# DeltaNet and soft-MoE slots: 32-token steps with wider matmul tiles and half as many matmuls

## The chip, the cores and the metric

The kernel runs on one core of one Trainium2 chip. The metric is device time in microseconds, as the median of several runs. The engines have short names throughout: PE is TensorE (matmuls; its weight loads are listed apart as PEld), DVE is VectorE, ACT is ScalarE, POOL is GpSimd, SP is SyncE, which here only issues DMAs.

## The reference

Two blocks follow each other. The first is a delta-rule attention with a state of 48x48 per batch and head, 4 batches, 8 heads, 768 tokens, all in 32-bit floats:

```python
k_n = k / (np.linalg.norm(k, axis=-1, keepdims=True) + 1e-06)
for t in range(S):
    kt, vt, bt = (k_n[:, :, t], v[:, :, t], beta[:, :, t, None])
    y[:, :, t] = np.einsum('bhd,bhde->bhe', q[:, :, t], state)
    v_old = np.einsum('bhde,bhd->bhe', state, kt)
    state = state + bt[:, :, :, None] * np.einsum('bhd,bhe->bhde', kt, vt - v_old)
```

Its output, as x of 3072 tokens by 384 features, goes through a mixture of experts with 32 slots (8 experts, 4 slots each, hidden width 1024):

```python
logits = x @ phi
d = softmax(logits, axis=0)          # over the tokens
slot_input = d.T @ x                 # 32 x 384, four rows per expert
slot_out[e] = relu(slot_input[e] @ w1[e]) @ w2[e]
c = softmax(logits, axis=1)          # over the slots
return c @ slot_out
```

(The two softmaxes stand here in short; the reference writes them out, with 1e-9 added to the sums.)

## The kernel before, in words

**Layout.** The partitions hold 4 batches x 32 tokens. A step is 32 tokens of all four batches and all eight heads; there are 24 steps, and four steps make a group, so there are 6 groups. Head vectors of 48 are padded with zeros to 64, so that two heads fill 128 partitions after a transpose. `e` counts pairs of heads, `g` the head in the pair, `b` the batch, `c` the step in its group, `m` the group.

**One step's preparation.** `load` (L315) brings K, Q and V, each with four DMAs of 48 KB on SP's queue, into rings of 11, 5 and 7 buffers. `turn` (L346, copied to X by ACT at L355) transposes K and Q. `products` (L373) multiplies K by K and K by Q, within each batch: 32 matmuls with tiles of 48x32. ACT copies the first to G (L385), DVE masks the second into AT (L389).

**One group's inversion.** `invert` takes the G of four steps: a 32x32 block transpose on DVE (lb, L404), norms, an elimination on POOL within blocks of 16 (L443, L447; on DVE for the first group), a transpose back to DT (L459) and to Dn (L461), and then two rounds of small matmuls that join the two halves of 16 tokens, `couple`: 128 matmuls each (L473, L478). ACT copies the first result to X16 (L486), DVE subtracts the second from DT (L493).

**One step's chain.** `chain` is the serial part. `state` multiplies the transposed K by the state St (R, L518), DVE subtracts this from V (L534), `solve` multiplies by DT (W, L544), ACT and DVE copy the result in two masked versions, one for even and one for odd batches, side by side into W (L557, L553), `update` adds K times W to the state, which stays in two banks of PSUM (S, L567; 64 tokens of two batches at a time), and ACT and DVE copy one bank each to St (L582, L579). Beside it run Q times the state (QS, L518) and the inner product AT times W (AU, L590), which give the output Y (L597). `state`, `solve` and `inner` are 32 matmuls each.

**Routing.** After each group `route` transposes Y (L615), forms logits (L628), updates a running maximum and the slot sums sacc (L688 to L698). At the end `experts` runs the slots through w1 (L863) and w2 (L903) and writes the output (L938 on). 24 pieces of w1 (512 KB) and 32 of w2 (384 KB) are loaded by SP at L755 into whatever buffer is free for good (`weights`, `home`, `place`), and into nine buffers `wx` of their own; the last w2 pieces overwrite w1 pieces that have been used.

**Order.** The program is emitted in an order that a planner finds by hand-written costs. `Plan.op` notes an operation with its engine, its time and what it reads and writes; `Plan.order` runs a list schedule and picks, among the ready operations of an engine, the one with the longest path behind it. It also models the clock of TensorE, by windows of TICK, and six free banks of PSUM. Each engine then runs its instructions strictly in the planned order. Every 32-bit matmul appears in the profile as two matmul records and two weight loads.

Of the kernel before, what the change touches and what calls it, by code (L numbers as in the profile page):

```python
# [15 lines left out]
class Op:  # L16
    __slots__ = ("eng", "us", "fn", "deps", "succ", "acq", "rel", "bias", "land", "tail", "start", "end", "left", "at", "name", "area")
# [9 lines left out]
class Plan:  # L27
# [9 lines left out]
    TICK, NEED = 3.413, 0.374  # L37

    def __init__(self, banks, limit):
        self.ops, self.writer, self.readers = [], {}, {}  # L40
        self.free = {b: 0.0 for b in range(banks)}
        self.limit = limit

    def op(self, eng, us, fn, r=(), w=(), acq=None, rel=None, pre=(), bias=0.0, land=0.0, name=""):
        o = Op()
        us, o.area = us if isinstance(us, tuple) else (us, 0.0)
# [40 lines left out]
    def order(self):  # L87
# [9 lines left out]
        tick, full, sums = 0, False, {}  # L97
        while len(done) < n:
            picks = []
            for eng, ls in ready.items():  # L100
# [15 lines left out]
                if cand:  # L116
                    first = min(c[0] for c in cand)
                    t, o = min(((t, o) for t, o in cand if t <= first + 1e-9), key=lambda c: (-c[1].tail, c[1].at))
                    picks.append((t, o.at, o))
# [16 lines left out]
            if o.eng == "PE":  # L136
                while (tick + 1) * self.TICK <= t:
                    full = sums.get(tick, 0.0) >= self.NEED * self.TICK
                    tick += 1
                us *= 1.0 if full else 2.0  # L140
                x, e = t, t + us
                while x < e:
                    k = int(x / self.TICK + 1e-9)
                    y = min(e, (k + 1) * self.TICK)
                    sums[k] = sums.get(k, 0.0) + o.area * (y - x) / us
                    x = y
# [28 lines left out]
def kernel(  # L175
# [56 lines left out]
    AT = ring(NA, [P, 2, HQ, C], "AT")  # L232
# [5 lines left out]
    DT = ring(2, [P, U, C], "DT")  # L238
    Dn = buf([P, U, C], "Dn")
    X16 = buf([P, U, QC], "X16")  # L240
    R = buf([P, H, D], "R")
    W = ring(2, [P, H, 2, D], "W")
    St = buf([P, 2, HQ, 2, D], "St")
# [16 lines left out]
    def pe(n, m, cols, conc, area=None):  # L260


        us = n * 2 * max(20, (2 * max(min(64, m), cols) + 12) / conc) / 2400
        return us, n * 2 * cols * 2 * (area or 1.0 / conc) / 2400

    def turns(n):
        return 0.113 * n, 128 * 2 * n / 2400
# [29 lines left out]
    tri = buf([P, C], "tri")  # L297
    nc.vector.tensor_reduce(tri, bdm.rearrange("p h t -> p t h"), axis=AX.X, op=ALU.add)
# [9 lines left out]
    nc.gpsimd.memset(Dn, 0.0)  # L308
    nc.vector.memset(bank[:, 6:8, :], 0.0)
# [50 lines left out]
    def products(n, which):  # L360
# [6 lines left out]
        def product():  # L367
            for e in range(HQ):
                for b in range(B):
                    for g in range(2):  # L370
                        r = slice(DP * g, DP * g + D)
                        rb = slice(C * b, C * b + C)
                        nc.tensor.matmul(  # L373
                            at(h, g)[rb, w * C * e:w * C * (e + 1)], lhsT=x[r, 0, e, rb],
# [3 lines left out]
        plan.op("PE", pe(32, 32, w * C, 6.0, 0.125), product,  # L378
                r=[("X", n % NX, i) for i in {0, *which}], w=[h], acq=h,
                pre=[("G", m % 2, c)] * (0 in which) + [("AT", n % NA)] * (1 in which), name="prod")  # L380
        for j, i in enumerate(which):
            ps = lambda j=j: at(h, 0, 2)[:, :, 0:w * C * HQ].rearrange(
                "p g (e j t) -> p g e j t", e=HQ, j=w)[:, :, :, j, :]
            if i == 0:
                plan.op("ACT", act(256), lambda ps=ps: nc.scalar.activation(  # L385
                    G[m % 2][:, H * c:H * c + H].rearrange("p (e g) t -> p g e t", g=2), ps(),
                    ACT.Copy), r=[h], w=[("G", m % 2, c)], rel=h, name="G")
            else:
                D_(dve(256, True), lambda ps=ps: nc.vector.tensor_tensor(  # L389
                    AT[n % NA], ps(),  # L390
                    tri.unsqueeze(1).unsqueeze(1).broadcast_to([P, 2, HQ, C]), op=ALU.mult),
                   r=[h], w=[("AT", n % NA)], rel=h, name="AT")

# [3 lines left out]
    def invert(m):  # L397
# [56 lines left out]
        for s in range(2):  # L454
# [3 lines left out]
                op=ALU.mult), r=["tt", "tt1", ("gm", z)], w=["tS"], name="tS")  # L458
        D_(dve(1024, False, 1.75), lambda: nc.vector.transpose(  # L459
            DT[z].rearrange("p u t -> p t u"), tS), r=["tS"], w=[("DT", z)], name="DT")  # L460
        D_(dve(512, False, 1.75), lambda: nc.vector.transpose(  # L461
            Dn.rearrange("p u s -> p s u")[:, 0:QC, :],
            tS.rearrange("p t s -> p s t")[:, 0:QC, :]), r=["tS"], w=["Dn"], name="Dn")

        hx, ht = Banks(1, "bulk"), Banks(1, "bulk")

        def couple(us, first):
            for u in us:
                for b in range(B):
                    r0 = C * b  # L470
                    if first:
                        r = slice(r0, r0 + C)
                        nc.tensor.matmul(at(hx)[r0:r0 + QC, QC * u:QC * u + QC],  # L473
                                         lhsT=gr[r, u, 0:QC], rhs=DT[z][r, u, QC:C],
                                         start=(u == 0), stop=True, skip_group_check=True)
                    else:
                        r = slice(r0, r0 + QC)
                        nc.tensor.matmul(at(ht)[r0:r0 + C, QC * u:QC * u + QC],  # L478
                                         lhsT=Dn[r, u, :], rhs=X16[r, u, :],
                                         start=(u == 0), stop=True, skip_group_check=True)  # L480

        for i in range(4):
            plan.op("PE", pe(32, 32, 16, 4, 0.0625),
                    lambda i=i: couple(range(8 * i, 8 * i + 8), True),
                    r=gk + [("DT", z)], w=[hx], acq=hx, pre=["X16"], name="X16")
        plan.op("ACT", act(512), lambda: nc.scalar.activation(  # L486
            X16.rearrange("p u t -> p (u t)"), at(hx), ACT.Copy), r=[hx], w=["X16"], rel=hx,
            name="X16")
        for i in range(4):
            plan.op("PE", pe(32, 32, 16, 4, 0.0625),  # L490
                    lambda i=i: couple(range(8 * i, 8 * i + 8), False),
                    r=["X16", "Dn"], w=[ht], acq=ht, name="T16")
        D_(dve(512, True), lambda: nc.vector.tensor_tensor(  # L493
            DT[z][:, :, QC:C], DT[z][:, :, QC:C], at(ht).rearrange("p (u t) -> p u t", t=QC),
            op=ALU.subtract), r=[ht, ("DT", z)], w=[("DT", z)], rel=ht, name="DT-")
# [11 lines left out]
    def chain(n):  # L507
        m, c = divmod(n, GC)
        x, kk, a, t = X[n % NX], K[n % NK], AT[n % NA], DT[m % 2]
        vn, ww, y = V[n % NV], W[n % 2], Y[m % 2]  # L510

        def state(h, i):
            for e in range(HQ):
                for b in range(B):
                    for g in range(2):
                        r = slice(DP * g, DP * g + D)
                        rb = slice(C * b, C * b + C)
                        nc.tensor.matmul(at(h, g)[rb, D * e:D * e + D], lhsT=x[r, i, e, rb],  # L518
                                         rhs=St[r, b // 2, e, b % 2, :], start=(e == 0),
                                         stop=(i == 0), skip_group_check=True)  # L520

        def halves(h):
            return at(h, 0, 2)[:, :, 0:HQ * D].rearrange("p g (e d) -> p g e d", d=D)
# [3 lines left out]
        hy, hw = Banks(2, "chain"), Banks(1, "chain")  # L527
        rhs = vn
        if n:
            hr = Banks(2, "chain")  # L530
# [488 lines left out]
```

## Time and profile before

| | |
|---|---|
| median of 3 runs | 475.68 us (467.55 to 477.08) |
| the profiled execution | 474.24 us, span 472.5 us |
| PE / PEld busy | 330.5 us (70%) / 253.2 us (54%), 12,438 records each |
| DVE / ACT / POOL busy | 135.2 / 103.8 / 95.1 us |
| mean granted clock of TensorE | 0.724 |
| moved by DMA | 45.89 MB, 97 GB/s over the span |
| DT- of the six groups (L493) starts at | 61.5, 123.8, 187.4, 246.7, 307.0, 360.7 us |
| the experts' matmuls (L842 on) start at | 412.0 us |

The span is the time from the first to the last instruction of the profiled execution. A line of the timeline gives start, duration, engine, source line, operation, output and inputs, the shape, and how many instructions were merged; in brackets stands how long the engine had been idle before and what ended this. "issue" there means that the profile shows nothing the engine waited for. A line of the windows gives the stretch and its length, then for PE, PEld, DVE, ACT and POOL the busy time and the number of instructions, then the granted clock, the DMA engines' busy share and GB/s.

### The profile page before, as it was taken

How to read it: one execution, taken by the hardware profiler on the slowest of the kernel's cores; microseconds unless marked ns; L12 is line 12 of the kernel's file. 1: busy time of each engine (PE TensorE's matmuls, PEld its weight loads, DVE VectorE, ACT ScalarE, POOL GpSimd, SP SyncE). 2: the span in 40 equal slices, each digit the busy share in tenths (PEclk: the TensorE clock that was granted, in tenths of full speed). 3: DMA queues.
4: the chain of work that ended last, by engine and by line, in shares of the span. 5: the costliest groups of instructions: out<-in, count | busy, mean ns of one | idle time of the engine just before them, and what ended most of it. 6: DMA issues, size and time to landing. Idle time of an engine off the chain costs nothing.

```text
span 472.5 us, 26509 instructions
## 1 busy us (share of the span) xinstructions
PE 330.5 (70%) x12438; PEld 253.2 (54%) x12438; DVE 135.2 (29%) x302; ACT 103.8 (22%) x200; POOL 95.1 (20%) x225
## 2 busy tenths in 40 slices
PE   3766546662767787857598767866877786799762
PEld 2544545552656666656477656655766674524221
DVE  3284314012313133231342415421122123311031
ACT  2322112121023221422222322201320132301021
POOL 8101552001083004800108304800000000000000
PEclk9999998665587656975756786555655568679985
DMA  4444444488233311223112223333241026229567
GB/s 76 83 82 89 77 85 74 81 221 241 55 56 65 58 22 21 50 41 55 29 31 38 65 65 111 93 108 94 92 135 42 6 69 204 68 74 401 227 184 216
DMA packets 91084, 45.89 MB, mean 97 GB/s; under 512 B 80656, under 2 KB 83792, under 8 KB 90976
## 3 DMA queue, kind: packets, MB, share of 16 engines
q1 hardware_dynamic: 88320, 41.70, 34.8%
q10 hardware_dynamic: 2368, 2.41, 1.8%
q8 instruction: 97, 1.59, 1.4%
q0 software_dynamic: 288, 0.10, 0.1%
q14 instruction: 11, 0.09, 0.1%
HBM read 39.47 MB, written 4.72 MB: 94 GB/s over the span
## 4 chain that ended last, share of the span: by engine, by line
PE 51%; issue 21%; DMA 9%; SPq 7%; DVE 4%; POOL 4%; ACT 3%; ACTq 0%; DVEq 0%; POOLq 0%
PE bank L518 7%; SPq L315 7%; PE bank L544 7%; PE bank L567 6%; PE bank L590 5%; PE bank L346 5%; PE bank L373 4%; PE bank L478 4%; PE bank L473 3%; PE bank L615 3%; DMA out_dram<-Y 2%; POOL tt L447 2%; DMA Qall<-in_moe_w_dram 2%; POOL pr L443 2%; PE bank L863 2%
## 5 line engine op out<-in xcount | busy, mean ns | idle before, releaser
L518 PE MATMUL bank<-St,X 48*32 48x48 f32 x2944 | 44.3, 245 | 36.8 <-issue 35.5
L518 PEld LDWEIGHTS bank<-St,X 48*32 48x32 f32 x2944 | 35.5, 125 | 42.1 <-issue 39.3
L544 PE MATMUL bank<-R,DT 32*32 32x48 f32 x1472 | 32.5, 256 | 12.4 <-issue 10.4
L553 DVE TENSOR_SCALAR W<-bank,par 128x384 f32<-128x384 f32 x24 | 14.8, 618 | 91.0 <-ACT W L557 90.6
L355 ACT ACTIVATE X<-bank 128x1024 f32<-128x1024 f32 (+1 forms) x28 | 25.2, 902 | 62.1 <-PE bank L346 57.0
L567 PE MATMUL bank<-W,Kall 64*48 64x96 f32 x736 | 33.2, 337 | 7.0 <-issue 5.5
L373 PE MATMUL bank<-X 48*32 48x64 f32 (+1 forms) x1792 | 28.9, 267 | 13.2 <-issue 12.0
L590 PE MATMUL bank<-W,AT 32*32 32x48 f32 x1536 | 33.2, 250 | 5.8 <-issue 5.0
L544 PEld LDWEIGHTS bank<-R,DT 32*32 32x32 f32 x1472 | 27.6, 145 | 16.6 <-issue 13.4
L590 PEld LDWEIGHTS bank<-W,AT 32*32 32x32 f32 x1536 | 28.4, 141 | 10.3 <-issue 7.9
L557 ACT ACTIVATE W<-bank,par 128x384 f32<-128x384 f32 x24 | 13.9, 580 | 90.2 <-PE bank L544 89.1
L373 PEld LDWEIGHTS bank<-X 48*32 48x32 f32 x1792 | 23.7, 134 | 18.6 <-issue 15.3
L478 PE MATMUL bank<-X,Dn 16*32 16x16 f32 x1536 | 24.2, 207 | 13.4 <-issue 13.4
L346 PE MATMUL bank<-ident,Qall 128*128 128x128 f32 x96 | 23.9, 397 | 13.1 <-DMA Qall<-in_q_dram 11.6
L567 PEld LDWEIGHTS bank<-W,Kall 64*48 64x48 f32 x736 | 25.5, 173 | 12.1 <-issue 8.4
L408 POOL TENSOR_TENSOR tt<-lb,low 128x256 f32<-128x256 f32 x12 | 8.6, 733 | 114.0 <-DVE lb L404 114.0
L346 PE MATMUL bank<-ident,Kall 128*128 128x128 f32 x96 | 24.6, 406 | 9.4 <-DMA Kall<-in_k_dram 7.9
L478 PEld LDWEIGHTS bank<-X,Dn 16*32 16x32 f32 x1536 | 22.5, 146 | 16.2 <-issue 15.7
L499 POOL TENSOR_TENSOR Vall<-Vall,nT 128x384 f32<-128x384 f32 x24 | 19.4, 826 | 48.5 <-DMA Vall<-in_v_dram 46.4
L473 PE MATMUL bank<-DT,G 32*16 32x16 f32 x1536 | 18.0, 183 | 12.4 <-issue 12.2
L579 DVE COPY St<-bank 112x384 f32<-112x384 f32 x23 | 12.8, 556 | 47.8 <-PE bank L567 47.8
L346 PEld LDWEIGHTS bank<-ident,Qall 128*128 128x128 f32 x96 | 17.7, 209 | 15.7 <-issue 14.3
(165 smaller groups left out, 462.5 us busy)
## 6 DMA issues: line engine op xcount, KB each, us to landing
Kall<-in_k_dram SPq DMA_DIRECT2D x96, 48.0 KB, 2.3
Qall<-in_q_dram SPq DMA_DIRECT2D x96, 48.0 KB, 3.1
Vall<-in_v_dram SPq DMA_DIRECT2D x96, 48.0 KB, 2.0
wx<-in_moe_w_dram SPq DMA_DIRECT2D x9, 512.0 KB, 7.1
wx<-in_moe_w_dram SPq DMA_DIRECT2D x9, 384.0 KB, 5.4
X<-in_moe_w_dram SPq DMA_DIRECT2D x7, 384.0 KB, 7.8
X<-in_moe_w_dram SPq DMA_DIRECT2D x5, 512.0 KB, 3.3
out_dram<-Y SPq DMA_DIRECT2D x24, 96.0 KB, 3.1
```

The source lines that it names most:

```text
L315: plan.op("SP", 0.42, lambda b=b, ap=ap: nc.sync.dma_start(out=dst[C * b:C * b + C, :, 0:D], in_=ap), w=[key + (b,)], pre=pre, land=0.35, ...
L346: nc.tensor.transpose(at(h, j)[:, P * e:P * e + P], src[:, P * e:P * e + P], ident)
L355: plan.op("ACT", act(512 * len(which)), lambda: nc.scalar.activation(dst, at(h, 0, 2) if len(which) > 1 else at(h).unsqueeze(1), ACT.Copy) ...
L373: nc.tensor.matmul(at(h, g)[rb, w * C * e:w * C * (e + 1)], lhsT=x[r, 0, e, rb], rhs=x[r, which[0]:which[0] + w, e, rb], start=(e == 0), s ...
L473: nc.tensor.matmul(at(hx)[r0:r0 + QC, QC * u:QC * u + QC], lhsT=gr[r, u, 0:QC], rhs=DT[z][r, u, QC:C], start=(u == 0), stop=True, skip_gro ...
L478: nc.tensor.matmul(at(ht)[r0:r0 + C, QC * u:QC * u + QC], lhsT=Dn[r, u, :], rhs=X16[r, u, :], start=(u == 0), stop=True, skip_group_check= ...
L499: plan.op("POOL", pool(384), lambda: nc.gpsimd.tensor_tensor(V[n % NV], V[n % NV], sm[m % 2]["nT"][:, H * c:H * c + H].unsqueeze(2).broadc ...
L518: nc.tensor.matmul(at(h, g)[rb, D * e:D * e + D], lhsT=x[r, i, e, rb], rhs=St[r, b // 2, e, b % 2, :], start=(e == 0), stop=(i == 0), skip ...
L544: nc.tensor.matmul(at(hw)[rb, D * u:D * u + D], lhsT=t[rb, H * c + u, :], rhs=rhs[rb, u, :], start=(u == 0), stop=True, skip_group_check=True)
L553: D_(dve(384, True), lambda src=src: nc.vector.tensor_scalar(ww[:, :, 1, :], src(), par[:, 1:2], None, op0=ALU.mult), r=[hw], w=[("W", n % ...
L567: nc.tensor.matmul(bank[DP * g:DP * g + D, SB + i, 2 * D * e:2 * D * e + 2 * D], lhsT=kk[r, 2 * e + g, 0:D], rhs=ww[r, 2 * e + g].rearrang ...
L590: nc.tensor.matmul(at(hy, g)[rb, D * e:D * e + D], lhsT=a[rb, g, e, :], rhs=ww[rb, 2 * e + g, b % 2, :], start=(n == 0 and e == 0), stop=True,
```

## The change

All operands keep their values; zeros are put between them so that one matmul does the work of two.

- `products`: two batches at a time, tiles of 48x64. The result holds also the products across the batches; ACT and DVE mask these out (G in three operations instead of one, AT over twice as many elements).
- `state`: both heads of a pair at once. St has a block for each head and zeros beside it; the moving operand is 96 wide, the contraction runs over all 128 partitions. R and QS take one bank each, not two.
- `solve` and `inner`: two batches at once, 64x64, with DT and AT as block-diagonal matrices. DT is copied by ACT (by DVE once) into DTb with the even batches in one half and the odd ones in the other; the inner product reads an unmasked copy of W, Wc, that ACT makes.
- `couple`: two heads at once, by Dn and X16 as block matrices and Gl, a packed copy of half of G.
- The state's copies: ACT takes the first head of each pair from both banks (partitions 0 to 47), DVE the second (64 to 111).
- The planner gets a model of instruction blocks (BLOCK, FETCH), a preference for matmuls that fill the array when it has lately been filled little, and a filler that is never set (`self.fill` stays None), so that its branch does nothing.
- NFREE, the number of buffers that only weights use, goes from 9 to 1; DTb, DT, AT and the second half of St become homes for weights.

```diff
+    BLOCK, FETCH = 128, 3.5
+    WINDOW, KEEP, DENSE, BONUS, FORCE = 2.5, 0.46, 0.5, 40.0, 0.46
...
+                    t, o = min(((t, o) for t, o in cand if t <= first + 1e-9), key=lambda c: (
+                        -c[1].tail - (bonus if eng == "PE" and c[1].area > self.DENSE * c[1].us else 0.0),
+                        c[1].at))
...
         def product():
             for e in range(HQ):
-                for b in range(B):
+                for i in range(2):
                     for g in range(2):
                         r = slice(DP * g, DP * g + D)
-                        rb = slice(C * b, C * b + C)
+                        rb = slice(2 * C * i, 2 * C * i + 2 * C)
                         nc.tensor.matmul(
-                            at(h, g)[rb, w * C * e:w * C * (e + 1)], lhsT=x[r, 0, e, rb],
+                            at(h, g)[rb, 2 * w * C * e:2 * w * C * (e + 1)], lhsT=x[r, 0, e, rb],
                             rhs=x[r, which[0]:which[0] + w, e, rb], start=(e == 0), stop=True,
                             skip_group_check=True)
...
+                plan.op("ACT", act(256), lambda ps=ps, dst=dst: nc.scalar.activation(
+                    dst, ps()[:, :, :, 0:C], ACT.Copy, scale=par[:, 0:1]), r=[h],
+                    w=[("G", m % 2, c)], rel=h, name="G")
+                for g in range(2):
+                    D_(dve(128, True), lambda ps=ps, dst=dst, g=g: nc.vector.scalar_tensor_tensor(
+                        dst[:, g], ps()[:, g, :, C:2 * C], par[:, 1:2], dst[:, g], op0=ALU.mult,
+                        op1=ALU.add), r=[h, ("G", m % 2, c)], w=[("G", m % 2, c)], rel=h, name="G")
...
+        plan.op(on, dve(512) if fast else pool(512, 2.5), lambda: eng.tensor_tensor(
+            tD, t[:, 0].rearrange("p i s -> p s i").unsqueeze(2).broadcast_to([P, QC, 2, QC]),
+            gmx.rearrange("p x s -> p s x").unsqueeze(3).broadcast_to([P, QC, 2, QC]),
+            op=ALU.mult), r=["tt", "tt1", "gmx"], w=["tD"], name="tD")
...
+        def couple(qs, first):
+            for q2 in qs:
                 for b in range(B):
+                    r = slice(C * b, C * b + C)
                     if first:
+                        nc.tensor.matmul(at(hx)[r, C * q2:C * q2 + C],
+                                         lhsT=Gl[r, 2 * q2:2 * q2 + 2].rearrange(
+                                             "p x i -> p (x i)"),
+                                         rhs=DT[r, 2 * q2:2 * q2 + 2, QC:C],
+                                         start=(q2 == 0), stop=True, skip_group_check=True)
                     else:
+                        nc.tensor.matmul(at(ht)[r, C * q2:C * q2 + C], lhsT=Dn[r, q2, :],
+                                         rhs=X16[r, q2].rearrange("p x j -> p (x j)"),
+                                         start=(q2 == 0), stop=True, skip_group_check=True)
...
+                plan.op("ACT", act(1024), lambda j=j: nc.scalar.activation(
+                    DTb[z][:, :, j, :], DT, ACT.Copy, scale=par[:, j:j + 1]), r=["DT"],
+                    w=[("DTb", z, j)], name="DTb")
...
         def state(h, i):
             for e in range(HQ):
                 for b in range(B):
-                    for g in range(2):
-                        r = slice(DP * g, DP * g + D)
-                        rb = slice(C * b, C * b + C)
-                        nc.tensor.matmul(at(h, g)[rb, D * e:D * e + D], lhsT=x[r, i, e, rb],
-                                         rhs=St[r, b // 2, e, b % 2, :], start=(e == 0),
-                                         stop=(i == 0), skip_group_check=True)
+                    rb = slice(C * b, C * b + C)
+                    nc.tensor.matmul(at(h)[rb, 2 * D * e:2 * D * e + 2 * D], lhsT=x[:, i, e, rb],
+                                     rhs=St[:, b, e].rearrange("p g d -> p (g d)"),
+                                     start=(e == 0), stop=(i == 0), skip_group_check=True)
...
         def solve():
             for u in range(H):
-                for b in range(B):
-                    rb = slice(C * b, C * b + C)
-                    nc.tensor.matmul(at(hw)[rb, D * u:D * u + D], lhsT=t[rb, H * c + u, :],
+                for i in range(2):
+                    rb = slice(2 * C * i, 2 * C * i + 2 * C)
+                    nc.tensor.matmul(at(hw)[rb, D * u:D * u + D],
+                                     lhsT=t[rb, H * c + u].rearrange("p j t -> p (j t)"),
                                      rhs=rhs[rb, u, :], start=(u == 0), stop=True,
                                      skip_group_check=True)
...
+        plan.op("ACT", act(384), lambda: nc.scalar.activation(
+            wc.rearrange("p u d -> p (u d)"), at(hw)[:, 0:H * D], ACT.Copy), r=[hw],
+            w=[("Wc", n % 2)], rel=hw, name="Wc")
...
+            for g in range(2):
+                r = slice(DP * g, DP * g + D)
+                src = bank[r, SB:SB + 2, 0:H * D].rearrange("p i (c d) -> p i c d", d=D)
+                dst = St[r].rearrange("p (i j) e g d -> p g i (j e) d", i=2)[:, g]
+                if g:
+                    D_(dve(768, True), lambda src=src, dst=dst: nc.vector.tensor_copy(dst, src),
                        r=["psS"], w=[("St", 1)], name="S")
                 else:
+                    plan.op("ACT", act(768), lambda src=src, dst=dst: nc.scalar.activation(
                         dst, src, ACT.Copy), r=["psS"], w=[("St", 0)], name="S")
...
-    NFREE = 9
+    NFREE = 1
```

## The prediction

> **What bounds the kernel now.** I read the page first (busy shares, chain, queues), then the timeline of the tensor engine alone, then the windows of one period, and last the handovers between the engines. The sum is made against the profiled execution, 474.2 us with a span of 472.5; the median of the runs, 475.7, stands 0.3% above it.
>
> ```profile
> PE 330.5 (70%) x12438; PEld 253.2 (54%) x12438; DVE 135.2 (29%) x302; ACT 103.8 (22%) x200; POOL 95.1 (20%) x225
> PEclk9999998665587656975756786555655568679985
> PE 51%; issue 21%; DMA 9%; SPq 7%; DVE 4%; POOL 4%; ACT 3%; ACTq 0%; DVEq 0%; POOLq 0%
> q8 instruction: 97, 1.59, 1.4%
> ```
>
> PE carries half of the chain that ended last, and another 21% (99 us) is "issue": PE stands, and nothing the profile shows holds it. 12,438 loads of weights and as many matmuls are 24,876 instructions; 97 packets of the instruction queue make 256 each, so one packet holds 128 pairs. The timeline of PE shows what the gaps are:
>
> ```profile
> 113.39 0.30 PE L478 MATMUL bank<-X,Dn 16*32 16x16 f32 x8
> 118.18 1.90 PE L478 MATMUL bank<-X,Dn 16*32 16x16 f32 x128 [4.49 <-issue]
> 121.91 1.80 PE L478 MATMUL bank<-X,Dn 16*32 16x16 f32 x120 [1.83 <-issue]
> 123.64 0.57 PE L567 MATMUL bank<-W,Kall 64*48 64x96 f32 x8
> 125.36 1.21 PE L567 MATMUL bank<-W,Kall 64*48 64x96 f32 x24 [1.15 <-issue]
> ```
>
> Between gaps lie exactly 128 pairs (the last 128 are 120 + 8), and PE restarts 3.73 and 3.45 us apart though it needs only 1.9 us for them. Over the trace, between 115 and 405 us, the instruction packets follow each other at a median of 3.67 us, 51 of 74 under 4.0. So PE works at the rate at which blocks of 128 pairs come in: a pair costs 29 ns however small its matmul is.
>
> [...]
>
> ```profile
> 187.00:247.00 60.00, 44.01 (x2037) 37.34 (x2032) 18.19 (x39) 15.65 (x31) 12.85 (x28) 0.70 0.23 41
> 247.00:307.00 60.00, 45.73 (x2010) 38.52 (x2006) 21.89 (x47) 15.85 (x30) 29.32 (x72) 0.67 0.29 75
> ```
>
> One period (four steps, one inversion, one routing) is 60 us: 44 us of PE and 16 us of gaps; 2,037 pairs are 15.9 blocks, times 3.67 = 58. DVE (18 to 22 us) and ACT (16) have room.
>
> **The matmuls.** Each 32-bit matmul is two records. Per step the state products fall from 128 records to 64, the solve and the inner product from 64 to 32 each, the products from 64 to 32; the couplings fall from 512 to 256 per period; update (32 per step), transposes and routing stay. A period has 4 x (64+32+32+32+32+8) + 256 + 55 = 1,111 pairs, 8.7 blocks, at least 32 us of fetching instead of 58.
>
> The array does not get less. Times per record, full clock / half clock, from starts in the timeline: update L567, 64x48 stationary with 96 columns, 25/46 ns; logits L628, 128x32 with 128 columns, 33/60; L590, 32x32 with 48, 12.7/22.4; L478, 32 stationary columns and 16 moving, 15.3 at half, while L473, 16 and 16, takes 10.2, so stationary columns count too; a transpose 130/237. Hence per period, full/half: state 256 records at L567's rate 6.5/11.7 (now 6.2/7.6); products 128 at L628's 4.2/7.7 (now 3.2/4.5); update 3.2/5.9; couplings 256 at 10/16 ns 2.6/4.1 (now 5.2/6.5); transposes of K and Q 4.1/7.6; routing 4.2/7.0. Solve and inner product now use 64 stationary columns and only the two tiles on the diagonal. No row shows that: the floor is today's 0.81/1.43 us each, the ceiling four times L478's per-record time at half for doubled columns, two abreast, 61 ns x 32 = 1.95 us at half; I take 0.95/1.9, near the ceiling since L478 shows the columns counting: 7.6/15.2 (now 6.5/11.2). Sum: **32.4 us at full clock, 59.2 at half** (now 32.6/50.3). Check on now: with full clock 30% of the time, 1/(0.3/32.6 + 0.7/50.3) = 43 us, and the window has 44.
>
> **The clock** therefore decides. In the trace it is 1.0 or 0.5 for stretches that are multiples of 3.41 us (the row's nines before 71 us stand for no record: there four transposes take 1.09 us, the half-clock time). For each such stretch I summed records x 2 x moving columns x the share of the array that the tile spans (32x32 one sixteenth, 64x64 a quarter, transposes whole), over 8,192 full-speed cycles. Next stretch at full: 7 of 65 below 0.25, 11 of 24 between 0.25 and 0.35, 11 of 11 above. The change doubles this sum for state, solve, inner product and products, since tiles are wider: 14.8 us of whole array per period become 20.3, and these fall into a shorter period. Scaling the stretches so, with a period of 45 us, 70% lie above 0.30 (58% at 52 us, 75% at 42). This supposes that zeros in the block-diagonal operands count like data. At 70%: 1/(0.7/32.4 + 0.3/59.2) = 37.5 us of PE.
>
> [...]
>
> **What still stands.** A coupling block of 128 small pairs takes 1.3 to 2.0 us against 3.67 of fetching: 2 us lost, twice: 4 us a period (0 if the order mixes them well, 8 if weight loads slow the fetch as at 113 us).
>
> **Handovers.** Two engines that read the same bank take turns; two that read different banks start together:
>
> ```profile
> 378.28 0.58 ACT L557 ACTIVATE W<-bank,par 128x384 f32<-128x384 f32 x1 [4.45 <-PE bank L544]
> 378.89 0.62 DVE L553 TENSOR_SCALAR W<-bank,par 128x384 f32<-128x384 f32 x1 [4.04 <-ACT W L557]
> 381.19 0.56 DVE L579 COPY St<-bank 112x384 f32<-112x384 f32 x1 [1.68 <-PE bank L567]
> 381.19 0.49 ACT L582 ACTIVATE St<-bank 112x384 f32<-112x384 f32 x1 [1.09 <-PE bank L567]
> ```
>
> The two state copies now read both banks, ACT on partitions 0 to 47, DVE on 64 to 111, 768 elements each: 0.81 (L948) and 0.96 us (L945). Whether different partitions of one bank take turns no row shows: 0.96 if not, 1.82 if so, against 0.56. I take the turns, since every same-bank pair that I looked at does. Behind the copies stand the next R matmuls, and behind these on PE everything later in the order. The step's chain is then R, W, S on PE 2.6 to 4.8 (3.0 at 70%), R on DVE 0.55, W 0.58 + 0.62, copies 1.8, seven handovers of 0.08: 7.1 us, 28 a period. PE's 41 us cover it, unless the fixed order puts too little between; 3.5 us a period for that (0 to 10).
>
> **Added work off the chain**, per period: DVE gets two G sums of 0.28 (L657) per step, AT 0.42 to 0.69 (L493), state copy +0.4, Dn, gmx and X16 1.3: +6.3, to 27 of 45. ACT: Wc 0.49 per step (queued behind W, ahead of the state copy, done while S runs), state copy +0.3, Gl and two DTb 2.7 less X16 0.6: +5.4, to 21. POOL: tD, two times 0.72 (L456). All lie under PE's 45; uncovered they would add some 13.
>
> **Ends.** The first group's DT- ends at 62: between 41 and 61 PE runs 5.6 blocks, then 2.8, 10 us less, but 2.5 us of DVE work come in, and PE at 61.7 waits 4.8 us for Qall; I take 57 (52 to 62). Eight of nine spare weight buffers go, so eight 512 KB loads that ran at 97 to 114 us move to the last two groups. That frees the first period of fetches slowed from 3.7 to 7 us (the 4.5 us gap above), and SP no longer issues them ahead of Qall and Kall; late, they compete with the rest: 4.2 MB at the tail's 217 to 400 GB/s, 10 to 19 us if wholly exposed, 0 if spread over 80 us. I take 3.
>
> **Sum**: 57 + first period 47 + four at 37.5 + 4 + 3.5 = 45, 180 + last stretch 43 (four chains of 7.5, routing 11 to 13; now 51) + tail 60.5 + 3 + 1.7 outside the span = **392**; I say 390. Steady periods of 41 to 50 and the ends' bounds make 360 to 425 its own range.
>
> **Rivals.**
> - The clock stays as it is, 30% full: PE 47 + 4 + 3.5 = 54 per period: 57 + 56 + 216 + 51 + 65 + 2 = 447. For it: zeros may not count, and couplings stay sparse; against: every stretch above 0.35 was followed by full clock.
> - The chain decides: in-turn copies, and an order that leaves PE idle behind them, 50 a period: 57 + 52 + 200 + 48 + 65 = 422. For it: the four lines above; against: PE's other work per step exceeds the chain's idle time.
> - Gaps don't follow the count of pairs: then only couplings and the freed weight loads are saved, about 465. Against it: the exact 128.
> - Slower: the clock stays at half. PE 59 + 4 + 3.5 = 66.5 a period: 62 + 66 + 266 + 57 + 65 + 2 = 518. It decides once the full share falls under 13% (59.2 and 32.4 mix to 53 us, plus 7 = today's 60). For it: the wide matmuls cost 59 against 50 at half clock; against: 30% now with less array in use.
>
> **Chances.** Forecast 0.56, clock as now 0.18, chain 0.13, gaps stay 0.07, slower 0.06. The fourth is split between a small gain and none. A change within 2% is about what cannot be told from none here: faster 0.90, same 0.04, slower 0.06. Predicted is the forecast's 390; the range 350 to 445 takes in the chain case and most of the second.
>
> **To check.** Instruction packets about 55; "issue" under 8% of the chain; granted clock in the periods about 0.85; periods 45 us; state copies of 0.81 and 0.96 in turn; PE busy falling below 290. A clock at 0.65 or under would make the forecast wrong, as would periods over 52 with gaps behind St.

## The result and the profile after

The changed kernel takes **357.2 us** (median of 4 runs, 356.3 to 363.3) against 473.9 us for the kernel before on the same chip: a ratio of 0.760, with a 95% interval of 0.750 to 0.769. The forecast was 390 with a range of 350 to 445. The profiled execution took 363.3 us with a span of 361.6; it lies 1.7% above the median, and the sums below are made against it.

The page of the changed kernel, the lines that answer to those of before:

```profile
PE 275.7 (76%) x6998; PEld 211.4 (58%) x6998; DVE 173.0 (48%) x372; ACT 131.4 (36%) x235; POOL 104.6 (29%) x231
PEclk9999755589899898789999997898989995899975
PE 39%; DVE 15%; DMA 14%; SPq 10%; ACT 10%; issue 8%; POOL 3%; ACTq 1%; DVEq 0%; POOLq 0%
q8 instruction: 55, 0.90, 1.1%
```

The 55 instruction packets are those of the prediction's list; the matmul records fall from 12,438 to 6,998. "issue", the time in which PE stands and nothing the profile shows holds it, has fallen from 99 us to 28. The clock row mostly stands at 9 or 8 where it mostly stood at 5 to 7. The chain that ended last is now spread over PE, DVE, ACT, loads and SP's queue: no single engine holds most of it any more.

The same in numbers, from the windows (stretch and its length; busy time and instructions of PE, PEld, DVE, ACT, POOL; granted clock, DMA share, GB/s). Each stretch goes from the first group's DT- to the experts' first matmul; first the kernel before, then the changed one:

```profile
61.50:412.00 350.50, 250.59 (x10855) 208.86 (x10855) 98.67 (x213) 81.81 (x163) 72.30 (x168) 0.66 0.33 80
```

```profile
59.60:302.10 242.50, 193.16 (x6013) 166.35 (x6013) 127.90 (x261) 106.23 (x196) 82.83 (x179) 0.90 0.45 110
```

Nearly all of the gain lies here: 350.5 us become 242.5. PE's busy time falls by 57 us, its idle time by 51 (100 to 49). The idle time has also changed its kind. Adding up PE's waits in these stretches by what ended them gives 86.9 us of "issue" and 6.9 us of waits for DVE and ACT in the kernel before, and 11.0 and 37.2 us in the changed one. Some of the longest rows (engine, line, what ended the wait: total us, times, longest), before and then after:

```profile
PE bank L518 <- issue: 35.5, 20, 4.1
PE bank L478 <- issue: 11.0, 6, 4.5
```

```profile
PE bank L656 <- DVE W L639: 7.8, 8, 4.5
PE bank L551 <- DVE DT L532: 7.4, 3, 3.5
PE bank L605 <- DVE St L669: 6.7, 9, 1.3
PE bank L605 <- issue: 3.1, 3, 1.3
```

The beginning (59.6 us, was 61.5) and the end (59.5 us, was 60.5) hardly move. The granted clock is 0.90 in place of 0.66; since both traces grant 1.0 or 0.5 and nothing between, that is full clock 80% of the time in place of about 30%.

Gaps in which PE waits for nothing but the next block are now rare and short. In PE's timeline a state product of 64 records is cut once, after record 63:

```profile
214.42 1.94 PE L433 MATMUL bank<-X 48*64 48x128 f32 x62
216.29 1.52 PE L605 MATMUL bank<-St,X 128*32 128x96 f32 x63
219.13 0.24 PE L605 MATMUL bank<-St,X 128*32 128x96 f32 x1 [1.32 <-issue]
219.31 1.02 PE L557 MATMUL bank<-X,Dn 32*32 32x32 f32 x96
```

The two copies of the state do take turns, although they read different partitions of the two banks: in none of the 23 steps do they overlap. Either may go first:

```profile
144.48 0.96 DVE L669 COPY St<-bank 48x768 f32<-48x768 f32 x1 [2.51 <-PE bank L656]
145.47 0.80 ACT L672 ACTIVATE St<-bank 48x768 f32<-48x768 f32 x1 [1.08 <-DVE St L669]
158.03 0.80 ACT L672 ACTIVATE St<-bank 48x768 f32<-48x768 f32 x1 [5.10 <-PE bank L656]
158.87 0.96 DVE L669 COPY St<-bank 48x768 f32<-48x768 f32 x1 [0.86 <-ACT St L672]
```

### The profile page after: what moved, and what is told of

Its sections match the earlier page's. It is cut to its first block, busy times and chain, and to the rows that moved or that the text cites. A ratio compares the mean times of both kernels' runs of the same rounds, so it can differ in the third digit from the quotient of the medians.

```text
span 361.6 us, 15724 instructions
## 1 busy us (share of the span) xinstructions
PE 275.7 (76%) x6998; PEld 211.4 (58%) x6998; DVE 173.0 (48%) x372; ACT 131.4 (36%) x235; POOL 104.6 (29%) x231
## 4 chain that ended last, share of the span: by engine, by line
PE 39%; DVE 15%; DMA 14%; SPq 10%; ACT 10%; issue 8%; POOL 3%; ACTq 1%; DVEq 0%; POOLq 0%
SPq L375 10%; PE bank L605 8%; PE bank L628 6%; PE bank L656 6%; DVE St L669 4%; DMA X<-in_moe_w_dram 4%; DMA out_dram<-Y 3%; PE bank L433 3%; ACT St L672 3%; PE bank L406 3%; PE bank L679 2%; DMA DTb<-in_moe_w_dram 2%; PE bank L955 2%; DVE W L639 2%; PE bank L551 2%
## 5 line engine op out<-in xcount | busy, mean ns | idle before, releaser
L605 PE MATMUL bank<-St,X 128*32 128x96 f32 x1472 | 40.4, 263 | 12.6 <-DVE St L669 6.7
L605 PEld LDWEIGHTS bank<-St,X 128*32 128x32 f32 x1472 | 33.9, 118 | 15.5 <-DVE St L669 8.1
L433 PE MATMUL bank<-X 48*64 48x128 f32 (+1 forms) x896 | 35.3, 304 | 6.4 <-DVE ATall L454 2.9
L433 PEld LDWEIGHTS bank<-X 48*64 48x64 f32 x896 | 28.7, 168 | 10.4 <-issue 4.7
L679 PE MATMUL bank<-Wc,ATall 64*64 64x48 f32 x768 | 31.0, 236 | 2.3 <-ACT Wc L647 1.9
L628 PE MATMUL bank<-R,DTb 64*64 64x48 f32 x736 | 27.9, 227 | 4.8 <-issue 1.9
L679 PEld LDWEIGHTS bank<-Wc,ATall 64*64 64x64 f32 x768 | 29.6, 153 | 3.2 <-ACT Wc L647 2.2
L628 PEld LDWEIGHTS bank<-R,DTb 64*64 64x64 f32 x736 | 24.9, 142 | 9.3 <-issue 4.1
L512 POOL TENSOR_TENSOR tt<-tt,pr 128x28 f32<-128x28 f32 (+6 forms) x70 | 24.7, 353 | 5.5
L508 POOL TENSOR_TENSOR pr<-tt 128x28 f32<-128x28 f32 (+6 forms) x70 | 23.6, 337 | 5.1
```

Of the source, the lines that this page charges most:

```text
L433: nc.tensor.matmul(at(h, g)[rb, 2 * w * C * e:2 * w * C * (e + 1)], lhsT=x[r, 0, e, rb], rhs=x[r, which[0]:which[0] + w, e, rb], start=(e ...
L508: eng.tensor_tensor(o, t[:, :, j, 0:j].unsqueeze(2).broadcast_to([P, 2, w, j]), t[:, :, j + 1:QC, j].unsqueeze(3).broadcast_to([P, 2, w, j ...
L512: eng.tensor_tensor(t[:, :, j + 1:QC, 0:j], t[:, :, j + 1:QC, 0:j], o, op=ALU.add)
L605: nc.tensor.matmul(at(h)[rb, 2 * D * e:2 * D * e + 2 * D], lhsT=x[:, i, e, rb], rhs=St[:, b, e].rearrange("p g d -> p (g d)"), start=(e == ...
L628: nc.tensor.matmul(at(hw)[rb, D * u:D * u + D], lhsT=t[rb, H * c + u].rearrange("p j t -> p (j t)"), rhs=rhs[rb, u, :], start=(u == 0), st ...
L679: nc.tensor.matmul(at(hy)[rb, D * u:D * u + D], lhsT=a[rb, u % 2, u // 2, :], rhs=wc[rb, u, :], start=(n == 0 and u == 0), stop=True, skip ...
```

## The experiments

Two causes were to be told apart for the gain: fewer instruction blocks to fetch, and a clock that opens because the tiles span more of the array. A third was that the planner's new order does it. The chips differ (the kernel before has a median of 474 us beside the first runs and of 466 to 468 beside the later ones), so I compare ratios to the kernel before on the same chip.

### The fetch by itself

```python
for i in range(320):
    for b in range(4):
        r, c = slice(32 * b, 32 * b + 32), 32 * (i % 16)
        nc.tensor.matmul(bank[r, 0, c:c + 16], lhsT=a[r, c:c + 32], rhs=a[r, c:c + 16], ...)
# then the same with 96 columns and 128 rows, then the small ones twice more
```

> Only streams of matmuls on a bare core, nothing of the reference: 2,560 records with 16 columns on 32x32 tiles, 2,560 with 96 columns on 128x32 tiles, 2,560 small ones again, and 2,560 small ones while 24 weight pieces of 512 KB are loaded. Fetch theory: small records come at about 28 ns each (128 in 3.5 to 3.7 us) whatever the clock, with gaps after multiples of 128, so 72 us for each small stream; wide ones at 23 ns of array time are fetch-bound too, 28 ns; with the weight loads beside them the small ones take 35 ns or more. Rival, the gaps in the kernel are something else (semaphores, queues): small records at 10 to 16 ns, 26 to 41 us a stream, no gaps, and no effect of the loads.

PE's timeline, pieces of the first small stream, then of the wide one, then of the second small one:

```profile
3.55 3.17 PE L30 MATMUL bank<-a 32*32 32x16 f32 x223 [3.55 <-DMA a<-in_moe_w_dram]
10.69 1.90 PE L30 MATMUL bank<-a 32*32 32x16 f32 x128 [3.97 <-issue]
15.52 1.90 PE L30 MATMUL bank<-a 32*32 32x16 f32 x128 [2.92 <-issue]
22.54 1.90 PE L30 MATMUL bank<-a 32*32 32x16 f32 x128 [5.12 <-issue]
...
115.03 2.84 PE L38 MATMUL bank<-a 128*32 128x96 f32 x128 [0.88 <-issue]
118.76 2.85 PE L38 MATMUL bank<-a 128*32 128x96 f32 x128 [0.88 <-issue]
...
203.69 1.90 PE L30 MATMUL bank<-a 32*32 32x16 f32 x128 [1.83 <-issue]
207.42 1.90 PE L30 MATMUL bank<-a 32*32 32x16 f32 x128 [1.83 <-issue]
```

With no other engine computing, the first stall comes after 223 records and the later ones after another 128 (once after three times that, where the wide stream begins), and from 40 us on PE restarts every 3.45 to 4.0 us (3.73 in the lines of the later streams), whether the block needs 1.90 us of PE at half clock or 2.84 at full. That is 29 ns a record, for small and wide alike; inside a block a small one takes 15 ns (1.90 us for 128), so it is the next block that comes late. The trace also has the packets of the instruction queue: all 77 restarts after "issue" come 1.2 to 1.6 us after the last such packet has landed. The same holds for all 60 such restarts in the trace of the kernel before and for all 10 in that of the changed one, so what PE waits for in these gaps is shown in the kernels themselves.

The weight loads did not run where I wanted them: nothing held them back, so they ran beside the first stream, from 3 to 40 us, at 343 GB/s. There the restarts are 4.6 to 7.0 us apart. So here a block costs 3.7 us with no loads beside it, and 4.6 to 7.0 under these.

### More records, same share of the array

```diff
-    nc.tensor.matmul(at(h)[rb, 2 * D * e:2 * D * e + 2 * D], lhsT=x[:, i, e, rb],
-                     rhs=St[:, b, e].rearrange("p g d -> p (g d)"), ...)
+    for g in range(2):
+        o = 2 * D * e + D * g
+        nc.tensor.matmul(at(h)[rb, o:o + D], lhsT=x[:, i, e, rb], rhs=St[:, b, e, g, :], ...)
```

(and likewise for the update and the products)

> The changed kernel with its state products, update and products each split into two matmuls of half the columns: 2,848 records more (9,846 in all, 77 blocks of 128), the same share of the array, the same order, about 5% more array time in these parts. Fetch theory: a period of the groups has 1,623 pairs, 12.7 blocks at 3.67 us, 46.5 us at least against 40.4 now, plus the coupling blocks; with longer periods the array is filled less and the clock falls somewhat: 395 to 420 us. Rival, the gain came from the clock alone and fetching does not matter: 360 to 365 us.

Measured: **407.8 us**, ratio 0.857 (0.849 to 0.864). The chain on the page of this kernel, and its window from the first DT- to the experts:

```profile
PE 48%; issue 13%; DMA 11%; DVE 10%; SPq 10%; ACT 6%; ACTq 0%; POOL 0%; POOLq 0%; DVEq 0%
```

```profile
62.20:348.70 286.50, 222.45 (x8732) 194.89 (x8732) 128.15 (x261) 106.40 (x195) 81.74 (x177) 0.86 0.38 94
```

A little over half of the removed records (2,848 of 5,440), put back without any new arithmetic, cost 51 us. "issue" is up to 13%. The rival, that fetching doesn't matter, asked for 360 to 365 and is out. But the 51 us are not all fetching. The stretch is 44 us longer than in the changed kernel: PE's waits on "issue" grow by 32 us (11.0 to 42.7), its busy time by 29, and its waits for DVE and ACT shrink by 17. The busy time grows because the clock falls from 0.90 to 0.86 and because two halves take longer than the whole (a state product's record takes 13.0 ns at full clock with 48 columns and 22.8 with 96). Nor is the period of 47.8 us close to its floor, as the expectation had it: the stretch has 1,455 pairs a period and not 1,623, which makes 42 us of fetching.

### Less of the array, same records

```diff
-    nc.tensor.matmul(..., lhsT=x[:, i, e, rb], rhs=St[:, b, e]..., ...)
+    nc.tensor.matmul(..., lhsT=x[0:DP, i, e, rb], rhs=St[0:DP, b, e]..., ...)
```

(and 32 rows of 64 in solve, inner product and update)

> The changed kernel with half the contraction rows left out in the state products (64 of 128: the second head of each pair), in solve and inner product and update (32 of 64: every second batch). Counts, columns, order and all other engines' work stay; only the share of the array falls, from 20.3 to about 15.2 us of whole array per period, nearly that of the kernel before (14.8). Clock-by-area theory: the granted clock in the periods drops from 90% to 70 or 75%, PE's work per period grows by 7 to 10 us, 390 to 420 us. Rival, what counts is that PE is occupied: clock and time stay, 355 to 362 us.

Measured: **402.2 us**, ratio 0.846 (0.840 to 0.851). Its window over the same stretch:

```profile
60.40:338.60 278.20, 258.18 (x6012) 224.81 (x6012) 128.08 (x261) 107.76 (x195) 81.54 (x179) 0.63 0.39 96
```

With as many records as the changed kernel (6,012) and the same work on every other engine, PE is busy for 258 us in place of 193 and the clock stands at 0.63 in place of 0.90; that is full clock 27% of the time. At each clock a record takes what it took (state products 23 and 42 ns, solve 33 and 59), so the longer busy time is the clock's. PE is occupied 93% of this stretch, more than in either kernel, and still gets the low clock. So occupied time isn't what opened the clock here; the share of the array that the tiles span is.

The prediction's sum over stretches of 3.41 us, records weighted by columns and by the share of the array, agrees when it is made again on the new traces. In the changed kernel full clock followed on 0 of 8 stretches with a sum below 0.25, on 5 of 11 up to 0.35, and on all 52 above. With half the rows it was 2 of 39, 4 of 25 and 16 of 18, though PE was occupied over 90% of 67 of these 82 stretches. I had expected a clock of 0.70 to 0.75: longer periods lower the share again, and I had not carried that far enough.

Putting back just over half of the records thus costs 51 us, and taking away the wide tiles' share of the array 45, of a gain of 117. Each leans on the other, so the two can't be added up exactly.

### One part put back

```diff
-    for i in range(2):
-        rb = slice(2 * C * i, 2 * C * i + 2 * C)
-        nc.tensor.matmul(at(hw)[rb, D * u:D * u + D],
-                         lhsT=t[rb, H * c + u].rearrange("p j t -> p (j t)"), ...)
+    for b in range(B):
+        rb = slice(C * b, C * b + C)
+        nc.tensor.matmul(at(hw)[rb, D * u:D * u + D], lhsT=t[rb, H * c + u, b % 2, :], ...)
```

(and the inner product likewise)

> The changed kernel with solve and inner product alone put back to 32x32 tiles, one batch each: 1,536 records more (8,534, 67 blocks), 1.3 us less of whole array per period. Fetch theory: 1,367 pairs a period, 10.7 blocks, 39 us of fetching just under today's 40.4, so gaps return in part, +2 to +5 us a period: 370 to 387 us. Rival, array time decides: these two took 1.07 us each at full clock as 64x64 and 0.81 as 32x32, 2 us a period less: 343 to 350 us.

Measured: **374.1 us**, ratio 0.789 (0.784 to 0.794), in the fetch theory's range. From its page:

```profile
PE 273.0 (73%) x8534; PEld 202.2 (54%) x8534; DVE 173.0 (46%) x372; ACT 132.0 (35%) x235; POOL 104.4 (28%) x231
PE 44%; DMA 14%; SPq 12%; issue 12%; DVE 9%; ACT 6%; POOL 1%; ACTq 1%; POOLq 0%; DVEq 0%
```

PE's busy time falls (273.0 us against 275.7), as the array-time rival says, but the chain's issue goes from 8% to 12% and the kernel is slower: between the first DT- and the experts PE's waits on "issue" are 35.8 us where they were 11.0. This is a cleaner test of the fetch than the split columns, since PE's busy time in that stretch is the same in both kernels (190 us) and the clock nearly so (0.89 and 0.90). A wider tile that costs more array time is the better trade here, because what it saves is the fetch.

### The planner

The kernel before with the new class `Plan`, and the changed kernel with the old one; nothing else is edited.

> The kernel before with the planner of the change alone (instruction blocks, preference for array-filling matmuls), all matmuls as they were. Theory that the fetch of blocks and the clock carry the change: 12,438 records stay 97 blocks, so at most the order gets a little better, 460 to 480 us on the first chip, ratio 0.97 to 1.01. Rival, a good part of the gain is the better order: ratio 0.90 to 0.95.

> The changed kernel's matmuls with the planner of before. Theory: most of the gain stays, ratio to the kernel before 0.76 to 0.80. Rival as for the last run: 0.83 to 0.90.

Measured: 474.6 us, ratio 1.017 (1.009 to 1.024), and 355.6 us, ratio 0.759 (0.752 to 0.766). The new planner does nothing measurable for the changed kernel, which has 0.760 on the same chip, and the kernel before comes out 1.7% slower with it, a little outside what I had written. The gain is not in the new planner.

### The early weight loads

```diff
+    late_x = [("X", 17 % NX, 0)] if keys[0][0] == "wx" and key[0] == "w1" else []
-    plan.op("SP", 0.42, lambda: nc.sync.dma_start(out=view, in_=src), w=keys + [key],
+    plan.op("SP", 0.42, lambda: nc.sync.dma_start(out=view, in_=src), r=late_x, w=keys + [key],
```

> The kernel before with its nine early loads of w1 (512 KB each, 97 to 114 us) planned after step 17, some 140 us later, nothing else changed. If big loads slow the fetch of instruction blocks: between 97 and 120 us the blocks come at 3.7 us instead of 5 to 7, the first period falls from 62 to 54 to 57 us, and part is given back where the loads now stand: 464 to 471 us. Rival, the gaps there have another cause: the first period stays at 62 and the time at 472 to 476 us.

The same instructions as in the prediction's lines from 113 to 125 us, now without the loads beside them:

```profile
107.10 0.30 PE L478 MATMUL bank<-X,Dn 16*32 16x16 f32 x8
108.60 1.91 PE L478 MATMUL bank<-X,Dn 16*32 16x16 f32 x128 [1.20 <-issue]
112.33 1.80 PE L478 MATMUL bank<-X,Dn 16*32 16x16 f32 x120 [1.82 <-issue]
114.05 0.57 PE L567 MATMUL bank<-W,Kall 64*48 64x96 f32 x8
```

The gap before the 128 is 1.2 us in place of 4.5, the blocks between 97 and 120 us come 3.3 to 4.5 us apart, and the first period falls from 62.3 to 54.1 us. The local mechanism is shown. The time is not: 465.1 us, ratio 0.997 (0.994 to 1.000), where 464 to 471 had been written for a chip on which the kernel before takes 474. The next two periods are 63.8 and 63.1 us (63.6 and 59.3 before, in a trace from the slower chip): at least part is given back there.

### The state's copies

```diff
-    for g in range(2):          # ACT: head 0 of both banks; DVE: head 1 of both banks
-        src = bank[r, SB:SB + 2, 0:H * D]...
+    for i in range(2):          # ACT: both heads of bank 0; DVE: both heads of bank 1
+        for g in range(2):
+            src = bank[r, SB + i, 0:H * D]...
```

> The changed kernel with the state copies cut otherwise: ACT copies both heads of the first bank, DVE both of the second, two instructions of 384 elements each in place of one of 768, in the same planned order. No bank has two readers, so the turns fall away: about 1.1 us from the end of the update to a whole state instead of 1.8, 0.7 a step, 17 us over 23 steps if wholly exposed. Theory that the chain is in part exposed (state copies are 7% of the chain that ended last): 344 to 353 us. Rival, PE's other work covers the chain: 355 to 358 us. If the banks are not what makes them wait, the copies still follow each other and the time does not fall.

Measured: 353.7 us, ratio 0.758 (0.754 to 0.762). The time lies at the end of what I had written for an exposed chain, but on this chip the kernel before takes 465.8 us, and against 0.760 the ratio shows no gain. So both versions ran once more, side by side:

> The changed kernel unchanged, as the partner on the same chip for the next run: ratio 0.755 to 0.768 to the kernel before.

> The state copies cut by bank, once more, now beside the changed kernel on one chip. The trace of its first run shows both copies at the same time and PE no longer waiting for them, periods of 38.7 against 40.4 us: 6 to 10 us off the end, ratio to the changed kernel 0.972 to 0.985. If the shorter chain only moves the waits to the loads and to W, 0.99 to 1.0.

In the timeline the copies now run together, and R follows (before, one whole copy stood behind the other):

```profile
165.26 1.14 DVE L671 COPY St<-bank 48x384 f32<-48x384 f32 x2 [1.03 <-PE bank L656]
165.56 0.98 ACT L673 ACTIVATE St<-bank 48x384 f32<-48x384 f32 x2
166.91 1.53 PE L605 MATMUL bank<-St,X 128*32 128x96 f32 x64
```

So cutting by bank ends the turns. It isn't quite a test of the bank alone, since the two copies then also write separate columns of St, where they had written interleaved ones; that ACT's copy to Wc, a tile of its own, also waits (0.68 us at 164.27) for DVE's copy to W out of the same bank speaks for the bank. On one chip the kernel takes 354.5 us with this edit, ratio 0.756 (0.751 to 0.762), and 355.7 us without, ratio 0.760 (0.755 to 0.765): no difference that can be told, and my second expectation of 0.972 to 0.985 between them fell. PE's waits for St go from 8.8 us to 2.4, but its waits for DVE's copy of W and for K loads grow (10.0 and 6.2 us, from 8.9 and 3.0).

### Loads on another queue

Half of the V loads of the first eight steps are issued by ACT (`nc.scalar.dma_start`) instead of SP.

> The changed kernel with half of the V loads of the first eight steps (16 DMAs) issued by ACT instead of SP. SP issues without a pause for the first 120 us, 0.47 us a DMA, and PE's order waits for Q loads at 52 to 57 us. If SP's queue sets the beginning, the first group's DT- moves from 59.6 to 53 to 56 us and the time to 350 to 354 us, less what the planner's other order does (some 3 us either way). Rival, the first inversion or ACT's 0.8 us an issue sets it: 356 to 360 us.

360.2 us, ratio 0.766 (0.761 to 0.771): no gain. DT- of the first group moved from 59.6 to 67.7 us, not to 53. The edit also changed the planner's order, and V loads landed late, so this tells nothing certain of SP's queue; what bounds the first 60 us stays open.

### What stands behind the waits for W

In the changed kernel DVE stands before the transpose to DT, which needs POOL's elimination, with W's copy behind it in its queue; PE then waits 4.5 us for that copy:

```profile
153.91 1.98 DVE L532 STREAM_TRANSPOSE DT<-tS 128x1024 f32<-128x1024 f32 x1 [5.40 <-POOL tS L521]
155.76 0.53 DVE L639 TENSOR_SCALAR W<-bank,par 128x384 f32<-128x384 f32 x1
156.35 1.53 PE L656 MATMUL bank<-W,Kall 64*48 64x96 f32 x32 [4.53 <-DVE W L639]
```

The planner believed POOL faster than it is. On top of the copies by bank:

```diff
-    plan.op(on, dve(n, False, 0.86) if fast else pool(n, 2.2),
+    plan.op(on, dve(n, False, 0.86) if fast else 0.28 + 0.0017 * n,
```

> The state copies cut by bank, and the planner told what POOL's elimination steps take in the trace (starts 0.33 us apart for 28 elements, 0.48 for 112; the planner had 0.17 and 0.36, some 4 us too little for an inversion). In the trace DVE stands at the transpose to DT, which waits for POOL, while W's copy is queued behind it, and PE waits 12 to 14 us in all for W. If the order is at fault, W's copies move ahead of that transpose, PE's waits for W fall under 5 us, and the time to 343 to 350 us, ratio 0.735 to 0.75. Rival, the wait only changes its place (loads, couplings): ratio 0.75 to 0.765.

Measured: **343.9 us**, ratio **0.737** (0.733 to 0.741), the fastest version. PE's waits between 60 and 300 us in the kernel with the copies by bank alone (engine, line, releaser, total us, times, longest):

```profile
PE bank L656 <- DVE W L639: 10.0, 9, 5.8
PE bank L656 <- ACT W L643: 4.5, 2, 3.8
```

and, between 55 and 300 us, with POOL's true costs:

```profile
PE bank L656 <- DVE W L639: 4.4, 6, 1.3
PE bank L656 <- ACT W L643: 2.2, 3, 1.2
```

14.5 us become 6.6, and the stretch from the first DT- to the experts goes from 233.3 to 224.8 us. My 5 us for these waits was a little too low.

## Why the prediction was right or wrong, point by point

- **The bound, and the count.** Right: 29 ns a pair holds on a bare core, 1,111 pairs a period were counted from the code, 55 packets came. Fetching isn't hidden here: the bare stream (a restart every 3.45 to 4.0 us), the solve put back to small tiles (35.8 us of "issue" for 11.0) and the packets that land 1.2 to 1.6 us before each restart all say so.
- **The array's time.** Right within a few per cent at full clock. State products and update measure 23 and 22 ns a record where L567's 25 was taken. The products come to 37 where L628's 33 was taken. The solve, which no row showed, takes 1.07 us at full clock and about 1.85 at half, the inner product 0.9 to 1.25 and about 1.85; 0.95 and 1.9 were taken. The solve's 1.07 us are 33 ns a record for 64 stationary and 48 moving columns, against 12.7 for 32 and 48. That the stationary columns set the price is my reading; no run changed them alone.
- **The clock.** Right in kind, too low in size: 70% of the time at full clock was taken, 80% came (a granted clock of 0.90; 0.85 followed from the 70%). The run with half the rows (0.63 at the same records) shows that the share of the array decides. The scale of the sum, in cycles a column and a stretch, is that of the planner's costs in the kernel; no trace counts cycles, and the bounds 0.25 and 0.35 hold on that scale alone. That zeros count like data, which I had only supposed, fits the traces: if the sum takes operands that are half zeros at half their share, full clock followed on 15 of 15 stretches of the changed kernel between 0.15 and 0.25 but only on 13 of 37 of the kernel before, while with the zeros counted in full the same bounds, 0.25 and 0.35, fit both kernels. No run puts data in their place.
- **The term that was mis-sized** is "37.5 us of PE" in a period. Measured: 193.2 / 6 = 32.2. Two corrections explain it. At 80% (the same in the later run of this kernel) the formula gives 1/(0.8/32.4 + 0.2/59.2) = 35.6. And between the first DT- and the experts there are 1,002 records a period, not 1,111, since the first group's products and couplings and part of the second group's products are done before; 35.6 x 1,002 / 1,111 = 32.1.
- **The gaps and waits.** 4 + 3.5 in the sum, 49.3 / 6 = 8.2 measured: right as a sum, but by luck. The gaps on "issue", taken as 4, are 1.8 a period; the waits for DVE and ACT, taken as 3.5, are 6.2. Of these only 1.5 are for St, the wait that I had in mind; W's copies (2.1) and the transpose to DT (1.2) were not in the sum at all.
- **The copies of the state.** Right that they take turns. Taking the turns away gives no measurable gain, since W and the loads take their place.
- **The ends.** 57 for the beginning, 59.6 came, within 52 to 62: there PE waits 16.6 us for loads of K and Q, and the run with V loads on ACT's queue didn't show what would shorten this. The late weights were given 3 us at the tail; it got 1 us shorter, so no cost shows there. That their early absence frees the first period is right in the trace (44.7 us; 47 was taken), and the run with late loads shows the mechanism in the kernel before.
- **Added work on DVE, ACT and POOL.** Costed at nothing on the path, and that was wrong: PE's waits for DVE and ACT went from 6.9 to 37.2 us, DVE and ACT are now 25% of the chain that ended last, and the last run takes 8 us of it back: W's copies behind the inversion's work in the same queue. The prediction named that cover for DVE's and ACT's total time only, not for their order.
- **Sum.** 57 + 270 + 65.2 = 392 was forecast; 59.6 + 242.5 + 59.5 + 1.7 = 363.3 is the profiled execution. Of the 29 us, 27.5 lie in the periods.
- **Rivals.** "Gaps don't follow the count" and "the clock stays" are each refuted by a run in which that one thing was put back: 408 and 402 us. The chain did not decide. The slower case needed full clock under 13%; the lowest that any run showed is 27%.

## What to carry to other kernels

Where PE's timeline shows idle "issue" after multiples of 128 pairs of weight load and matmul, count the pairs: each cost 29 ns of fetching here. Merging matmuls paid where the wider ones took less extra array time than the fetch they saved: for the solve 32 pairs fewer, 0.93 us of fetching, against 0.26 us more of the array at full clock (1.07 for 0.81). Wide tiles paid a second time through the clock (0.90 granted in place of 0.66), even though half of what some of them multiply is zeros. And after such a change the cheap engines' queues want another look: a planned order is only as good as the costs it was given.

## What the runs showed of the hardware that I had not expected

- The time between instruction blocks in the bare streams was the same at half clock (the second small stream, 0.52 granted) and at full (the wide one, 1.00): 3.45 to 4.0 us. Under weight loads at 343 GB/s it was 4.6 to 7.0 us.
- The clock followed the share of the array that the tiles span, not PE's busy time: with half the rows PE was busy 93% of its stretch at a granted clock of 0.63, in the changed kernel 80% at 0.90.
- The two copies from the same banks were kept apart even on disjoint partitions (0.80 and 0.96 us, one behind the other). The profile puts the wait down to the other copy's semaphore; whether the chip needs it was not tried.
